# An unused tile of 128 bytes in front of the later working tiles of a two-layer linear-attention and MLP kernel

## The chip, the cores and the metric

The kernel runs on one core of a Trainium2 chip. A core has a matrix engine (TensorE, PE in the profile), three engines for elementwise work (VectorE or DVE, ScalarE or ACT, GpSimd or POOL), and SyncE (SP), which here issues the DMAs. Operands of matmuls lie in SBUF, a memory of 128 partitions in which a tile has one start address for all partitions; results go to PSUM banks. The metric is the time of one execution in microseconds on the device. A matmul reads two operands: the stationary one, which a weight load (PEld in the profile) puts into the array, and the moving one, which streams past it.

## The reference

The input x has 2048 rows of D = 448. Two kinds of block alternate, twice:

```python
def _A_ref(x, wqkv, wo):          # 16 heads of 28
    q, k, v = ...                 # from x @ wqkv
    phi = lambda t: jnp.where(t > 0, t + 1, jnp.exp(t)) + 1e-6
    pq, pk = phi(q), phi(k)
    kv = einsum("bhsd,bhse->bhde", pk, v)
    z = einsum("bhsd->bhd", pk)
    o = einsum("bhqd,bhde->bhqe", pq, kv) / (einsum("bhqd,bhd->bhq", pq, z) + 1e-6)
    return o @ wo
def _B_ref(x, w1, b1, w2, b2):    # F = 1792
    return gelu(x @ w1 + b1) @ w2 + b2

x = x + _A_ref(layernorm(x), wqkv, wo)
x = x + _B_ref(layernorm(x), w1, b1, w2, b2)
# and both once more, with the same weights
```

## The kernel before, in words

All data is float32. A product of two float32 matrices is computed as three one-pass products of type float32r: each operand is split into a high part (a cast, on ACT) and a low part (the rest, on DVE or POOL), and high x high, high x low and low x high are summed in PSUM. The last chunk of 64 columns puts high and low parts into the two halves of 128 rows and needs two products instead of three. A few small products (the sums over rows, the combination of kv with the weights, and the transposes) are plain float32.

Each of the two layers has three stages. The first phase goes over 16 tiles of 128 rows: layernorm, transposition, split into XH and XL, then the products psk (k, function `proj`, L306 to L311), psq (q, same lines) and G (L481 to L485), which accumulates the normalized x against phi(k). The transition forms M from G, wv and wo (kvp, L641; mp, L651), and the first block's attention output and layernorms (o_mm, L732 to L734, whose moving operands are Mh and Ml). The MLP stage goes over four blocks of 512 rows; each has 14 steps. A step computes hp (`mlp1`, L801 to L805: 11 matmuls, stationary w1h, w1l or w1x, moving XH or XL, 512 columns that lie as four runs of 128), gelu, a split into gh and gl, and then y for the step before (`mlp2`, L819 to L821: 12 matmuls, stationary gh or gl, moving w2h or w2l, 448 columns). Between them stand the attention outputs of the next block (op, `oc_mm`, L743 to L747: stationary qh or ql, moving the pieces of M, which live in tiles of the q weights). The order on every engine is written out by hand (ORDER, STEPS, LAUNCH, PLAN) and nothing reorders it.

Tiles come from pools. A pool places its tags in SBUF one behind the other, in the order in which a tag is first asked for; each tag has a fixed number of buffers, and a buffer's size is rounded up to 32 bytes. The pool `consts` comes first, then `wts` with w1h, w1l, w1x, w2h and w2l, then `work`: nine x tiles (tag H) of 1,792 bytes per partition, five tiles of 4,096 bytes (tag S), then the statistics of the layernorm (bst, bmv, bve, brs, three buffers each of at most 24 bytes of content), two tails of 512 bytes, and then all others: the pieces of the k and q weights (tags W0 to W6 and V0 to V6, used later for pq, pz and M), XH and XL (8,192 bytes, two of each), and A, B, E, F, e and xn of 2,048 bytes, from which the split operands xnh, xnl, qh, ql, gh, gl, kh and kl are taken. The last ones are the small denominators dn and rd.

In the built program w1h, w1l, w1x, w2h and w2l start 64 bytes past a multiple of 256, as do the x tiles and the S tiles; rows inside the weights are multiples of 256 bytes apart, so every slice that a product takes keeps that offset. The statistics end at 143,040, which is 192 past a multiple of 256. The tails and everything behind them up to dn have sizes that are multiples of 256 and so start at 192 too.

The program's first calls are these; the tags bst to brs are first asked for in `ln_stats` under `stage_a`, and the tag of the tails in `stage_n`:

```python
    stage_a(0, 0)
    bn = ln_bn(xt[0, 1])
    stage_n(0, 0)
```

Of the kernel before, what the change touches and what calls it, by code (L numbers as in the profile page):

```python
# [9 lines left out]
F32 = mybir.dt.float32  # L10
# [12 lines left out]
def linear_attn_mlp_kernel(  # L23
# [28 lines left out]
    work = ctx.enter_context(tc.tile_pool(name="work", bufs=2))  # L52
# [138 lines left out]
    def ln_bn(xs):  # L191
        st = work.tile([128, 6], F32, name="bst", tag="bst", bufs=3)
        dve.bn_stats(st, xs)
        return st

    def ln_stats(xs, st=None):
        st = ln_bn(xs) if st is None else st
        mv = work.tile([128, 2], F32, name="bmv", tag="bmv", bufs=3)
        dve.bn_aggr(mv, st)
        ve = work.tile([128, 1], F32, name="bve", tag="bve", bufs=3)  # L200
        dve.tensor_scalar(ve, mv[:, 1:2], 1e-5, None, op0=OP.add)  # L201
        rs = work.tile([128, 1], F32, name="brs", tag="brs", bufs=3)
        pool.tensor_tensor(rs, ve, mhalf, op=OP.pow)  # L203
        return xs, mv, rs
# [172 lines left out]
    def stage_a(l, t):  # L377
        sts[l, t] = ln_stats(xt.pop((l, t)))

    def stage_n(l, t):  # L380

        xs, mv, rs = sts.pop((l, t))
        dve.tensor_scalar(xs, xs, mv[:, 0:1], rs, op0=OP.subtract, op1=OP.mult)
        xns[l, t] = xs
        if t < TURNED[l]:
            d = tails[l, t] = work.tile([128, 128], F32, name="tail", tag="tail", bufs=2)
            act.copy(d.rearrange("p (u n) -> p u n", u=2), xs[:, None, TL:].to_broadcast([128, 2, 64]))
# [521 lines left out]


    stage_a(0, 0)
    bn = ln_bn(xt[0, 1])
    stage_n(0, 0)
    split_hi("k", 0, st_k)
# [4 lines left out]
    for l in range(LAYERS):  # L919
# [27 lines left out]
        for tok in ORDER.split():  # L947
            name, j = tok.rstrip("0123456789"), int("0" + tok.lstrip("abcdefghijklmnopqrstuvwxyzQTG"))
# [69 lines left out]
```

## Time and profile before

| | |
|---|---|
| median of 3 runs | 885.9 us (885.64 to 886.61) |
| the profiled execution | 884.81 us |
| its span, first to last instruction | 883.1 us |
| granted clock of TensorE | 1.000 |
| TensorE busy, matmuls | 877.8 us, 4182 records |
| of these y (L819 to L821) | 1344 |
| hp (L801 to L805) | 1232 |
| psk, psq, G | 352 each |
| op (L743 to L747) | 264 |
| VectorE, ScalarE, GpSimd busy | 489.9, 343.5, 220.8 us |

A row of a group gives an engine's instructions of one line of the code. Ends of matmuls are modelled in the profile, and matmuls overlap, so the distance from one start to the next (called pitch below) says what a matmul costs while TensorE is never idle; starts are in the view in order of time. In tile names buffer numbers are left out: y<-w2h,gh is a matmul into y from w2h (moving) and gh (stationary).

### The profile page before, as it was taken

How to read it: one execution, taken by the hardware profiler on the slowest of the kernel's cores; microseconds unless marked ns; L12 is line 12 of the kernel's file. 1: busy time of each engine (PE TensorE's matmuls, PEld its weight loads, DVE VectorE, ACT ScalarE, POOL GpSimd, SP SyncE). 2: the span in 40 equal slices, each digit the busy share in tenths (PEclk: the TensorE clock that was granted, in tenths of full speed). 3: DMA queues.
4: the chain of work that ended last, by engine and by line, in shares of the span. 5: the costliest groups of instructions: out<-in, count | busy, mean ns of one | idle time of the engine just before them, and what ended most of it. 6: DMA issues, size and time to landing. Idle time of an engine off the chain costs nothing.

```text
span 883.1 us, 11676 instructions
## 1 busy us (share of the span) xinstructions
PE 877.8 (99%) x4182; PEld 773.0 (88%) x4182; DVE 489.9 (55%) x953; ACT 343.5 (39%) x603; POOL 220.8 (25%) x250
## 2 busy tenths in 40 slices
PE   9999999999999999999999999999999999999998
PEld 8999888888888888888899998988888888888887
DVE  6878585658455443226477876864664373433112
ACT  5676635334323322333356565332232233233221
POOL 5566532335013102012222344210320140130000
PEclk9999999999999999999999999999999999999999
DMA  5475637633313402051146543352332423111001
GB/s 157 135 231 165 199 88 211 180 99 118 131 59 104 154 0 96 1 178 48 48 133 192 164 127 105 113 171 79 116 106 84 136 72 108 49 48 42 1 1 42
DMA packets 63482, 94.76 MB, mean 107 GB/s; under 512 B 8896, under 2 KB 58560, under 8 KB 63424
## 3 DMA queue, kind: packets, MB, share of 16 engines
q1 hardware_dynamic: 63424, 94.01, 34.0%
q8 instruction: 33, 0.54, 0.3%
q14 instruction: 25, 0.20, 0.1%
HBM read 56.17 MB, written 34.60 MB: 103 GB/s over the span
## 4 chain that ended last, share of the span: by engine, by line
PE 96%; DMA 1%; DVE 1%; ACT 1%; issue 0%; SPq 0%; POOL 0%; DVEq 0%; ACTq 0%; POOLq 0%
PE y L820 10%; PE y L821 10%; PE y L819 10%; PE hp L801 9%; PE hp L803 9%; PE hp L802 9%; PE hp L805 3%; PE hp L804 3%; PE psq L308 2%; PE psq L307 2%; PE psq L306 2%; PE psk L307 2%; PE G L482 2%; PE G L483 2%; PE psk L308 2%; PE G L481 2%
## 5 line engine op out<-in xcount | busy, mean ns | idle before, releaser
L811 DVE TENSOR_TENSOR gl<-g,gh 128x512 fp32r<-128x512 f32 x112 | 83.1, 742 | 306.3 <-ACT gh L810 306.3
L807 ACT ACTIVATE g<-hp,b1s 128x512 f32<-128x512 f32 x112 | 77.2, 689 | 412.5 <-PE hp L805 409.2
L820 PE MATMUL y<-w2l,gh 128*128 128x448 f32 x448 | 164.6, 367 | 0.0
L821 PE MATMUL y<-w2h,gl 128*128 128x448 f32 x448 | 164.0, 366 | 0.0
L819 PE MATMUL y<-w2h,gh 128*128 128x448 f32 x448 | 162.9, 364 | 0.0
L801 PE MATMUL hp<-XH,w1h 128*128 128x512 f32 x336 | 132.8, 395 | 0.0
L803 PE MATMUL hp<-XL,w1h 128*128 128x512 f32 x336 | 132.4, 394 | 0.0
L802 PE MATMUL hp<-XH,w1l 128*128 128x512 f32 x336 | 132.1, 393 | 0.0
L203 POOL TENSOR_TENSOR brs<-bve,mhalf 128x1 f32<-128x1 f32 x64 | 39.5, 617 | 286.5 <-DVE bve L201 283.4
L820 PEld LDWEIGHTS y<-w2l,gh 128*128 128x128 f32 x448 | 84.1, 188 | 10.1
L819 PEld LDWEIGHTS y<-w2h,gh 128*128 128x128 f32 x448 | 84.1, 188 | 9.8
L821 PEld LDWEIGHTS y<-w2h,gl 128*128 128x128 f32 x448 | 84.2, 188 | 6.1
L803 PEld LDWEIGHTS hp<-XL,w1h 128*128 128x128 f32 x336 | 63.1, 188 | 15.1 <-issue 0.5
L802 PEld LDWEIGHTS hp<-XH,w1l 128*128 128x128 f32 x336 | 63.6, 189 | 11.7
L801 PEld LDWEIGHTS hp<-XH,w1h 128*128 128x128 f32 x336 | 63.0, 188 | 11.8
L810 ACT CAST gh<-g 128x512 fp32r<-128x512 f32 x112 | 69.6, 622 | 3.6
L694 POOL TENSOR_TENSOR pz<-pq,zb 128x448 f32<-128x448 f32 x32 | 36.8, 1154 | 87.2 <-DVE dn L700 76.1
L416 POOL TENSOR_TENSOR xnl<-x,xnh 128x384 fp32r<-128x384 f32 x32 | 35.1, 1095 | 71.7 <-ACT xnh L415 39.6
L296 DVE TENSOR_TENSOR XL<-sp,XH 128x512 fp32r<-128x512 f32 x50 | 44.4, 894 | 4.2 <-ACT XH L295 4.2
L805 PE MATMUL hp<-XL,w1x 128*128 128x512 f32 x112 | 44.4, 397 | 0.0
L804 PE MATMUL hp<-XH,w1x 128*128 128x512 f32 x112 | 44.0, 393 | 0.0
L763 POOL TENSOR_TENSOR x<-x,b2b 128x448 f32<-128x448 f32 x32 | 42.0, 1332 | 0.0
(146 smaller groups left out, 1565.0 us busy)
## 6 DMA issues: line engine op xcount, KB each, us to landing
x<-in_A_x_dram SPq DMA_DIRECT2D x32, 224.0 KB, 3.8
pq_d<-eq SPq DMA_DIRECT2D x32, 224.0 KB, 2.9
pq<-pq_d SPq DMA_DIRECT2D x32, 224.0 KB, 3.2
sq_m<-sq SPq DMA_DIRECT2D x14, 512.0 KB, 2.8
sp<-sq_m SPq DMA_DIRECT2D x56, 128.0 KB, 3.0
x<-x_d SPq DMA_DIRECT2D x32, 224.0 KB, 3.4
sq_a<-sq SPq DMA_DIRECT2D x12, 512.0 KB, 2.9
sp<-sq_a SPq DMA_DIRECT2D x48, 128.0 KB, 3.1
```

Of the source, the lines that this page charges most:

```text
L296: eng.tensor_tensor(lo.rearrange("p (c i n) -> p c i n", c=4, n=32), x, f(h), op=OP.subtract)
L801: pe.matmul(o, w1h[:, c, s], x.moving(x.hi, c), start=(c == 0), stop=False)
L802: pe.matmul(o, w1l[:, c, s], x.moving(x.hi, c), start=False, stop=False)
L803: pe.matmul(o, w1h[:, c, s], x.moving(x.lo, c), start=False, stop=False)
L804: pe.matmul(o, w1x[:, s], x.moving(x.hi, 3), start=False, stop=False)
L805: pe.matmul(o, w1x[:, s], x.moving(x.lo, 3), start=False, stop=True)
L807: act.activation(g, hp, AF.Gelu_apprx_tanh, bias=b1s[:, i:i + 1])
L810: act.copy(gh, g)
L811: dve.tensor_sub(gl, g, f(gh))
L819: pe.matmul(acc[j], gh[:, s], w2h[:, i], start=first, stop=False)
L820: pe.matmul(acc[j], gh[:, s], w2l[:, i], start=False, stop=False)
L821: pe.matmul(acc[j], gl[:, s], w2h[:, i], start=False, stop=last)
```

## The change

One line is added behind the first call of `stage_a`. It takes a tile of 32 float32 numbers per partition, 128 bytes, under a tag of its own, and nothing reads or writes it:

```diff
     stage_a(0, 0)
+    work.tile([128, 32], F32, name="space", tag="space", bufs=1)
     bn = ln_bn(xt[0, 1])
     stage_n(0, 0)
     split_hi("k", 0, st_k)
```

In the built program the tile stands between the statistics and the tails, and all that follows starts 128 bytes later: the tails at 143,168, which is 64 past a multiple of 256, and so on. The instructions of every engine, their order and their semaphores are the same as before.

## The prediction

> **What bounds the kernel now.** I read the page's head first, then the chain, then the groups by tile, then the order of time.
>
> ```profile
> span 883.1 us, 11676 instructions
> PE 877.8 (99%) x4182; PEld 773.0 (88%) x4182; DVE 489.9 (55%) x953; ACT 343.5 (39%) x603; POOL 220.8 (25%) x250
> PEclk9999999999999999999999999999999999999999
> ...
> PE 96%; DMA 1%; DVE 1%; ACT 1%; issue 0%; SPq 0%; POOL 0%; DVEq 0%; ACTq 0%; POOLq 0%
> ```
>
> TensorE is busy for 877.8 of 883.1 us at the full granted clock, and 96% of the chain that ended last is its matmuls. So only two things can move the end: the distance from one matmul's start to the next (the pitch, below), or a new wait. Waits of TensorE hardly exist: its view of waits lists 1.1 us for the first warm-up and 0.2 us in one G. The next views are the groups by tile: shortest/median/longest duration in ns, then first and last start.
>
> ```profile
> L819 PE MATMUL y<-w2h,gh x448: 358/364/373, 144.3 to 878.5; 128*128 128x448 f32 x150
> L820 PE MATMUL y<-w2l,gh x448: 358/367/373, 144.5 to 878.7; 128*128 128x448 f32 x150
> L821 PE MATMUL y<-w2h,gl x448: 358/368/373, 144.7 to 878.9; 128*128 128x448 f32 x150
> ```
> ```profile
> L743 PE MATMUL op<-wq,qh x72: 365/369/369, 169.3 to 768.2; 128*128 128x448 f32 x72
> L744 PE MATMUL op<-wq,qh x72: 362/365/366, 169.5 to 768.4; 128*128 128x448 f32 x72
> L745 PE MATMUL op<-wq,ql x72: 362/365/369, 169.7 to 768.6; 128*128 128x448 f32 x72
> ...
> L746 PE MATMUL op<-wq,qh x24: 365/365/365, 171.1 to 768.8; 128*128 128x448 f32 x24
> L747 PE MATMUL op<-wq,ql x24: 365/365/365, 171.3 to 769.0; 128*128 128x448 f32 x24
> ```
> ```profile
> L801 PE MATMUL hp<-XH,w1h x336: 390/392/404, 139.1 to 873.0; 128*128 128x512 f32 x168
> L804 PE MATMUL hp<-XH,w1x x112: 392/392/398, 141.3 to 873.8; 128*128 128x512 f32 x112
> ```
>
> These rows are a comparison that the kernel already contains. The op products run between the y products, in the same stage, with the same shape and the same neighbours on the other engines; but both operands of op (wq streamed; qh or ql loaded as weights) start 192 bytes past a multiple of 256, while y streams w2 from 64 past one and loads gh or gl from 192. The op durations lie in 362 to 369 ns, those of y in 358 to 373: twice as wide, and somewhat longer in the middle. The addresses of the operands do show in TensorE's time, by a little.
>
> Durations are modelled; pitches are not. In order of time (start, duration in us):
>
> ```profile
> 301.38 0.39 PE L803 MATMUL hp<-XL,w1h 128*128 128x512 f32 x1
> 301.61 0.39 PE L804 MATMUL hp<-XH,w1x 128*128 128x512 f32 x1
> 301.84 0.40 PE L805 MATMUL hp<-XL,w1x 128*128 128x512 f32 x1
> 302.08 0.36 PE L819 MATMUL y<-w2h,gh 128*128 128x448 f32 x1
> 302.28 0.36 PE L820 MATMUL y<-w2l,gh 128*128 128x448 f32 x1
> 302.48 0.37 PE L821 MATMUL y<-w2h,gl 128*128 128x448 f32 x1
> 302.69 0.36 PE L819 MATMUL y<-w2h,gh 128*128 128x448 f32 x1
> ```
>
> Starts are 0.20 to 0.24 us apart. Differencing the starts of the whole trace, in ns: y 203.8 (1,343 pitches); op with both operands at 192, 203.25 (264); the k, q and G products of the first phase, also 192 and 192, 203.1 without the pitches over 233, which are waits; hp 232.1 (1,232). The group means say the same: y 365.7 (the mean of 364, 367 and 366), op 365.5, hp 394.2, each its pitch plus 162.
>
> **The change, part by part.** The tile is never written or read, so no instruction, transfer or wait is added, and every engine and queue keeps its order. What moves is addresses. Before the new tile lie the twelve statistics buffers, 32 bytes apart, ending at 192 past a multiple of 256; every later tile up to the last four denominators' (dn, rd) is a multiple of 256 long. The 128 bytes take all of these from 192 to 64: tails, W and V pieces, XH, XL, A, B, E, F, e, xn. w1, w2, the x tiles and the S tiles stay at 64.
>
> So products fall in three classes: mixed 64/192 that become equal (y 1,344, hp 1,232, and 80 of the o products of block 0, whose Mh and part of Ml sit in S tiles), and equal 192/192 that become equal 64/64 (1,336: k, q, G, op and 16 of the o products).
>
> 1. y and the 80 o products: 203.8 to the 203.25 of op, 0.55 ns x 1,424 = 0.8 us gained. All of it is on the path, since TensorE does nothing else.
>
> 2. hp has no row with equal operands, so it is bounded. For what 64 more columns cost I take the two fp32 products: mp, 448 wide, has a pitch of 375.5 ns and kvp, 112 wide, 98.4, so 0.825 ns a column; a y column costs 203.8/448 = 0.455, little over half, so I take half of 0.825, 0.412, or 26.4 ns for 64 columns. If hp with equal operands is op plus that, its pitch is 203.25 + 26.4 = 229.65, and 2.45 ns x 1,232 = 3.0 us is gained. If instead the pitch grows in proportion to the width, 203.25 x 512/448 = 232.3, hp already runs as an equal product would and nothing is gained. Between: op's 0.55 ns, the only price of the offset seen on anything, gives 0.7 us. What is then left above y plus 26.4 (232.1 - 230.2 = 1.9 ns) is due to the offset or to hp's stream in four runs of 128; I give half of it to each, 0.95 ns x 1,232 = 1.2 us. I take 1.9 us, ends 0 and 3.0.
>
> 3. The 1,336 equal products: 192/192 to 64/64. Nearest row: the first-phase ones agree within 0.5 ns whether their operands lie at 192 or at 448 past a multiple of 512. I take nothing; ends are 0.55 ns either way, 0.7 us gained or lost.
>
> 4. The fp32 transposes: the four slices of tq start at 192, 128, 64 and 0 and pitch 108 to 113 ns in any of them. Nothing.
>
> 5. Copies, splits and sums on DVE, ACT and POOL, and the DMAs into W and V: cover is TensorE's own work. One step of the MLP lasts 11 x 232.1 + 12 x 203.8 = 5.0 us against 0.69 + 0.62 + 0.74 = 2.05 us of gelu, copy and split. If that cover were gone it would show as the waits of TensorE above, which hold 1.3 us. Only up to 13 us and where the phases change (around 94, 104 and 537 us) TensorE waits, some 4 us in pitches over 233 together. Loads of tiles at 64 and of tiles at 192 both occur now (x 3.4 us, pq 3.2 us to landing). A tenth of the 4 us either way bounds it; I take nothing.
>
> Sum: -0.8 - 1.9 = -2.7 us. The profiled execution took 884.8 us, its span of 883.1 and 1.7 around it; the change makes it 882.1 with a span of 880.4. It was 1.1 below the median of 885.9 (its runs lie from 885.6 to 886.6), so against that median I say 883.2.
>
> The rows show the neighbour in address mattering by 0.55 ns. [...]
>
> **The rivals.**
>
> A. Nothing measurable. The offset is worth only the 0.8 us of step 1, or op's 203.25 owes something else (its weights change every three products, its stream never repeats a tile at once). For it: the proportional reading of step 2, and 0.55 ns on 203 is small. Against: the doubled spread of y. Time 885.9 - 0.8 + 0.7 to 885.9 - 0.8, say 885.3.
>
> B. Slower: hp's long slot multiplies. Its longest durations, 404 ns against a median of 392, are no scatter. An hp product sums over four chunks of the width of x; the first matmul of the third chunk (L801, c=2) pitches 240.1 in the mean, those of the first two chunks 229.0; so at some distances between stream and weights one matmul in eleven pays 11 ns. With another distance all three chunks may hit it: 2 x 11 x 112 = 2.5 us lost. With step 1's gain of 0.8 that is 887.6. It decides from one added long slot in each step on, 1.2 us, which already eats step 1. Against: equal operands are calmer where they can be seen.
>
> C. More: the long slot goes as well and 64/64 is better than 192/192 too (step 3's end): 885.9 - 0.8 - 3.0 - 0.7 = 881.4. No row has 64/64 products.
>
> D. The change does not do what it says, the tile landing elsewhere or being dropped: addresses as built exclude it, so it gets nothing.
>
> **How the numbers follow.** 0.2%, 1.8 us, is about what a measurement of this kernel can tell from no change. Forecast, hp gaining between 1.0 and 3.0 us: 0.45, 882.1 to 884.1. A: 0.33, all within 0.2%. B: 0.15, half of it over 887.7 or near it, half inside 0.2%. C: 0.07. Faster by over 0.2% is then the forecast, C, less a part that scatters over the edge: 0.49. Slower: half of B and a rest for absolute offsets that I don't see, 0.12. Same: 0.39. The range leaves a tenth out at each end: below, most of C, with 0.3 us for the runs' scatter, 881.5; above, the worse part of B, 887.4. The forecast's own range is 881.8 to 884.4.
>
> **What would show it.** Right: the y rows narrow to about 362 to 369 and their mean falls from 365.7 to 365.2; hp's mean falls from 394.2 to about 392.7, its 404s disappear; op, psk, psq and G stay at 365; no wait of TensorE grows; counts are equal. A is right if y and hp keep their means within 0.3 ns. B is right if L801 gets longer in more chunks. The forecast is wrong above all if hp's excess belongs to its four separate runs of columns and not to its addresses, or if the class 64/64 behaves unlike 192/192.

## The result and the profile after

The changed kernel took 878.7 us (median of six runs; 877.8 to 880.6) against 885.4 us before (now six runs, too; the 885.9 above was the median of three): a ratio of 0.993, 95% interval 0.9915 to 0.9945. That is faster, and by two and a half times what was forecast (6.7 us against 2.7), outside the range. The profiled execution took 877.8 us, its span 876.1.

The head of the page and TensorE's waits after:

```profile
span 876.1 us, 11676 instructions
PE 870.8 (99%) x4182; PEld 771.5 (88%) x4182; DVE 489.0 (56%) x953; ACT 343.3 (39%) x603; POOL 220.8 (25%) x250
```
```profile
PE warm L157 <- DVE ones L152: 1.1, 1, 1.1
PE tp L246 <- DVE x L383: 0.3, 1, 0.3
```

Counts are the same, TensorE still fills the span, and its waits come to 1.4 us against 1.3. Its busy time fell by 7.0 us, as the span did. The groups by tile after (shortest/median/longest duration in ns):

```profile
L819 PE MATMUL y<-w2h,gh x448: 362/365/369, 143.5 to 871.5; 128*128 128x448 f32 x150
L820 PE MATMUL y<-w2l,gh x448: 362/365/369, 143.7 to 871.7; 128*128 128x448 f32 x150
L821 PE MATMUL y<-w2h,gl x448: 362/365/369, 143.9 to 871.9; 128*128 128x448 f32 x150
```
```profile
L801 PE MATMUL hp<-XH,w1h x336: 387/389/396, 138.3 to 866.1; 128*128 128x512 f32 x168
L804 PE MATMUL hp<-XH,w1x x112: 389/389/389, 140.5 to 866.8; 128*128 128x512 f32 x112
```

y narrowed from 358 to 373 down to the 362 to 369 that op had before. hp lost its long slots of 404, and its median fell from 392 to 389; L804 has one duration only. In order of time, a step of hp after:

```profile
302.16 0.39 PE L801 MATMUL hp<-XH,w1h 128*128 128x512 f32 x1
302.39 0.40 PE L802 MATMUL hp<-XH,w1l 128*128 128x512 f32 x1
302.62 0.39 PE L803 MATMUL hp<-XL,w1h 128*128 128x512 f32 x1
302.85 0.39 PE L801 MATMUL hp<-XH,w1h 128*128 128x512 f32 x1
303.08 0.39 PE L802 MATMUL hp<-XH,w1l 128*128 128x512 f32 x1
303.31 0.39 PE L803 MATMUL hp<-XL,w1h 128*128 128x512 f32 x1
303.53 0.39 PE L801 MATMUL hp<-XH,w1h 128*128 128x512 f32 x1
303.76 0.39 PE L802 MATMUL hp<-XH,w1l 128*128 128x512 f32 x1
```

Two decimals hide the pattern; the mean distances of starts over all 112 steps show it. The three matmuls of the first chunk are 231.0, 233.2 and 230.1 ns apart, the next two 228.1 and 227.9, and the last six settle at 226.4 to 227.0. Before, the step never settled: 228.8 to 233.1 all along, and 240.1 at the first matmul of the third chunk.

Pitches (distance of starts, in ns, means over the whole trace; single pitches over 250 at 448 columns and over 260 at 512, some 30 that stand at waits, behind float32 products or at the start of a phase, left out):

| products | before | after |
|---|---|---|
| hp, 1,232 | 232.0 | 228.2 |
| y, 1,344 | 203.8 | 202.7 |
| op, 264 | 203.25 | 202.3 |
| psk, psq, G | 203.0, 203.6, 202.8 | 203.0, 203.7, 203.1 |

With those put back, hp's pitches sum to 286.0 us before and 281.5 after, those of all 448-wide float32r products to 565.4 and 563.6. That is 4.5 + 1.8 = 6.3 us. The other 0.7 of the 7.0 lies ahead of the first product of k, which started at 6.8 us instead of 7.4, and is no part of the change: the first hp, at 139.1 us before and 138.3 after, started at 138.3 too with w1 and w2 moved alone (below), which gained nothing, and at 139.2 with everything moved, which gained as much as the change.

### The profile page after: what moved, and what is told of

Read it like the earlier page. It is cut to its first block, busy times and chain, and to the rows that moved or that the text cites. A ratio compares the mean times of both kernels' runs of the same rounds, so it can differ in the third digit from the quotient of the medians.

```text
span 876.1 us, 11676 instructions
## 1 busy us (share of the span) xinstructions
PE 870.8 (99%) x4182; PEld 771.5 (88%) x4182; DVE 489.0 (56%) x953; ACT 343.3 (39%) x603; POOL 220.8 (25%) x250
## 4 chain that ended last, share of the span: by engine, by line
PE 98%; DVE 0%; DMA 0%; POOL 0%; ACT 0%; issue 0%; DVEq 0%
PE y L821 10%; PE y L819 10%; PE y L820 10%; PE hp L802 9%; PE hp L803 9%; PE hp L801 9%; PE hp L805 3%; PE hp L804 3%; PE psk L307 2%; PE G L482 2%; PE psq L306 2%; PE psq L307 2%; PE psq L308 2%; PE G L481 2%; PE G L483 2%; PE psk L308 2%
## 5 line engine op out<-in xcount | busy, mean ns | idle before, releaser
L804 PE MATMUL hp<-XH,w1x 128*128 128x512 f32 x112 | 43.6, 389 | 0.0
L193 DVE BATCH_NORM_STATS2 bst<-x 128x6 f32<-128x448 f32 x64 | 39.9, 624 | 4.8 <-DMA x<-in_A_x_dram 3.7
```

The lines of the kernel that those rows point to most:

```text
L804: pe.matmul(o, w1x[:, s], x.moving(x.hi, 3), start=False, stop=False)
```

## Experiments

"Difference" below is the start of the moving operand less the start of the stationary one, modulo 256 bytes. hp had 128 before (192 and 64), and y had 128 too (64 and 192); the change makes both 0.

### Is it the place modulo 256? Other lengths of the tile

```diff
-    work.tile([128, 32], F32, name="space", ...)
+    work.tile([128, 64], F32, name="space", ...)     # 256 bytes; 96: 384; 16: 64; 48: 192
```

256 bytes:

> The tile has 256 bytes instead of 128: everything behind it moves, but keeps its place modulo 256. Theory 1 (what counts is the difference of the starts of the moving and the stationary operand modulo 256): as before the change, ratio 1.000 (885.4 us), y durations 358 to 373 ns, mean 365.7, hp mean 394.2. Theory 2 (the place as such matters: a period longer than 256, or a distance between tiles): a ratio below 0.996 or above 1.004. Theory 3 (any tile between the statistics and the rest separates them and that is what helps): 0.993.

384 bytes:

> 384 bytes: the same place modulo 256 as with the change, another modulo 512. Theory 1: as with the change, ratio 0.993 (878.7 us), y mean 365.3, hp 390.6. Theory 2: anything else; with a period of 512 bytes not 0.993.

64 bytes:

> 64 bytes: the later tiles start at multiples of 256, 64 below the offset of w1, w2. Theory 1 in its strict form (only equal offsets help): ratio 1.000 or above, hp mean 394 or more. Theory 1 by distance (half the distance, half the loss): about 0.9965 (882 us), hp mean near 392.4. Products with both operands among the later tiles (op, psk, psq, G) stay at 365 to 366 by either.

192 bytes:

> 192 bytes: the later tiles start 64 above the offset of w1, w2. Strict form: ratio 1.000 or above, hp mean 394 or more. By distance: about 0.9965, and equal to the tile of 64 bytes. If the sign of the difference matters (stationary ahead of or behind the moving operand) this and the tile of 64 bytes differ by more than 0.002.

| tile | difference hp, y | ratio to before (95%) | hp | y | psk, G |
|---|---|---|---|---|---|
| 256 | 128, 128 | 1.0002 (0.9993 to 1.0012) | 232.0 | 203.8 | 204.0, 203.7 |
| 384 | 0, 0 | 0.9921 (0.9906 to 0.9935) | 228.15 | 202.8 | 202.9, 203.1 |
| 64 | 192, 64 | 0.9997 (0.9988 to 1.0007) | 233.2 | 201.2 | 205.0, 204.6 |
| 192 | 64, 192 | 0.9988 (0.9979 to 0.9997) | 230.6 | 202.4 | 206.1, 205.8 |

A tile of 256 bytes left hp, y and the total as they were, and one of 384 did what 128 does: 256 bytes more moved hp and y by no more than 0.1 ns, and separating the tiles is not the cause. But the last two rows don't follow theory 1 in either form. y was faster with the difference 64 (201.2) than with 0 (202.7), so equal was not best for it. The sign mattered, too: hp has 233.2 and 230.6, y 201.2 and 202.4 with the same two differences the other way round. The two totals hide this; they differ by 0.0009, less than the 0.002 that was to tell. And psk and G, whose two operands stay equal, got 2 to 3 ns slower, and 1 ns slower even with 256 bytes, where no tile's place modulo 256 has moved. So these two hung on something else as well, which comes up again below.

### Difference or place? w1 and w2 moved, too

```diff
+    wts.tile([128, 32], F32, name="wpad")
     w1h = wts.tile([128, 3, F], F32R, name="w1h")
```

This alone:

> A tile of 128 bytes ahead of w1 instead: w1, w2, x and S at 192, all later tiles at 64. The later tiles have the places of the change, but hp and y stay mixed, the other way round (hp streams from 64 and loads from 192; y streams from 192 and loads from 64). If the difference decides: as before, 885.0 us, ratio 1.000, hp 232, y 203.8. If the place of XH, XL, A and B decides: as with the change, 0.993.

With the tile of the change as well:

> Both tiles: everything at 192, as far behind each other as with the change. If the difference decides: ratio 0.993, hp 228.2, y 202.7. If the place at 64 decides: 1.000. Products at equal offsets were up to 2 ns slower at 0 and 128 than at 64 and 192, so a part may hang on the place modulo 128, which is the same for 64 and 192.

Alone: ratio 0.9999 (0.9989 to 1.0008). With both: 0.9932 (0.9917 to 0.9947). The hp groups of the two:

```profile
L802 PE MATMUL hp<-XH,w1h x336: 390/392/404, 138.3 to 872.3; 128*128 128x512 f32 x168
L805 PE MATMUL hp<-XH,w1x x112: 392/392/398, 140.5 to 873.0; 128*128 128x512 f32 x112
```
```profile
L802 PE MATMUL hp<-XH,w1h x336: 387/389/397, 139.2 to 867.0; 128*128 128x512 f32 x168
L805 PE MATMUL hp<-XH,w1x x112: 389/389/389, 141.4 to 867.7; 128*128 128x512 f32 x112
```

The first (all later tiles at 64, as with the change, but w1 at 192) is the kernel before again, with its 404s; the second, with everything at 192, is the changed kernel. Slot by slot along the step the means agree within 0.2 ns with those of the kernel they resemble. For hp and y the difference counted here and not the place: with 192/64 in place of 64/192 the time was that of before (0.9999), with 192/192 in place of 64/64 that of the change (0.9932 against 0.993).

### One kind of product at a time

```diff
         xn = xns.pop((l, t))
+        if (l, t) == (0, 0):
+            work.tile([128, 32], F32, name="space2", tag="space2", bufs=1)
         h = t512("A", 2, "xnh", F32R)
```

With the tile of the change (hp equal, y mixed):

> The tile of the change, and a second one of 128 bytes ahead of A: XH, XL, W and V at 64 as with the change, A, B, E, F and e back at 192. hp is equal (64/64), y mixed (64/192), op mixed, psk and psq equal, G equal at 192. If the pitch belongs to each product's own two operands: hp 228.2 ns, y 203.8, gain against before 1,232 x 3.8 = 4.7 us, about 880.4, ratio 0.9947. If the neighbours or the place of the whole decide, hp does not get its 228.

Without it (y equal, hp mixed):

> Only the tile of 128 bytes ahead of A: A, B, E, F and e at 64, XH, XL, W and V at 192 as before. y equal (64/64), hp mixed. By own operands: y 202.75 ns, hp 232.0, gain 1,344 x 1.05 = 1.4 us, about 883.7, ratio 0.9984; the gains of this run and of the one with hp alone add up to that of the change (6.1 us of pitches).

Ratios 0.9979 (0.997 to 0.9989) and 1.0034 (1.0021 to 1.0047). Neither expectation held. With hp equal alone hp pitched 229.8, not 228.2: the seventh to tenth matmul of its step are at 226.6 to 226.9, as with the change, but the six ahead of them, behind the mixed y, at 228 to 236. With y equal alone y pitched 204.7, slower than the mixed 203.8, and the first phase rose as well: psk to 206.25, psq to 205.0, G to 205.7, though both operands of psk lie just where they lay before. Its groups there, and those before:

```profile
L306 PE MATMUL psk<-wk,XH x96: 362/368/473, 7.5 to 534.7; 128*128 128x448 f32 x96
L307 PE MATMUL psk<-wk,XH x96: 362/368/475, 7.8 to 534.9; 128*128 128x448 f32 x96
```
```profile
L306 PE MATMUL psk<-wk,XH x96: 362/365/467, 7.4 to 531.8; 128*128 128x448 f32 x96
L307 PE MATMUL psk<-wk,XH x96: 358/365/473, 7.8 to 532.0; 128*128 128x448 f32 x96
```

So a product's own two addresses did not fix its pitch (psk: 203.0 before, 206.25 here); what ran around it had a say.

### w1l alone moved away

```diff
+    wts.tile([128, 32], F32, name="lpad0")
     w1l = wts.tile([128, 3, F], F32R, name="w1l")
+    wts.tile([128, 32], F32, name="lpad1")
     w1x = wts.tile([128, F], F32R, name="w1x")
...
+    work.tile([128, 32], F32, name="space", tag="space", bufs=1)
```

> The changed kernel with w1l alone moved to 192 (128 bytes ahead of it and 128 behind). In hp, L801 streams XH while the w1l for L802 is being loaded; L802 has the w1l as its own weights and streams XH while the w1h for L803 is loaded. If a stream collides with the load that runs under it, L801 gets longer (from 227 ns in the steady chunks to 229 or more) and L802 does not. If a product's own pair decides, L802 gets longer and L801 does not. If both or all three change, the pattern of the whole step decides. y stays at 202.7. Whole: 0.994 to 0.996.

Ratio 0.9958 (0.9943 to 0.9973). In the second and third chunk the product ahead of w1l went from 228.1 and 226.8 to 231.7 and 232.1, the one with w1l from 227.9 and 227.0 to 233.4 and 233.8, the third from 226.5 and 226.4 to 227.6 and 227.7; the fourth chunk, where w1l has no part, stayed at 226.6 and 226.7. The product ahead of w1l, under which w1l is loaded (in the profile after the load starts 2 to 4 ns behind that product's start and takes 188 ns), paid 4 to 5 ns and the one that uses it 6 to 7, and the loop was back within 1.3 ns right behind them. (In the first chunk, which had not settled, the one with w1l fell from 233.2 to 231.8.) By the expectation this is the third case, the pattern of the whole step; which of the two reads, stream or load, is held up is not told by it.

### Do the four runs of hp's stream cost anything?

```diff
-            return x.rearrange("p (t c n) -> p t c n", t=4, c=4)[:, :, c]
+            return x.rearrange("p (c t n) -> p c t n", t=4, c=4)[:, c]
```

On the kernel before:

> The kernel before, with hp streaming one run of 512 columns of XH or XL in place of four runs of 128 (it takes 512 neighbouring columns, which are other elements, so what hp computes is changed; the sizes, the counts and the offset 192 stay). If half of hp's excess belongs to the four runs, as the prediction took it, hp falls from 232.0 to about 231 ns. If it is all the offset, hp stays at 232.0. If it is all the runs, about 230.

On the changed kernel:

> The same edit (hp computes with other elements of XH and XL) on the changed kernel, offset 64. If the runs cost something with equal offsets too, hp falls from 228.2 below 227.5; if they cost nothing, it stays at 228.2, of which the first chunk holds 231 and the rest 227.

In one execution of each, hp pitched 232.0 and 228.2, as without the edit. The four runs cost nothing that shows; what hp lost with the change was the offset's.

### Series of equal products, without neighbours

```diff
+    def series(n, cols, k, at, width=128):
+        o = bank("m", 2, "sr")
+        for i in range(n):
+            pe.matmul(o[:width, :cols], st4[:, at + k * 8:at + k * 8 + width], mv4[:, at:at + cols],
+                      start=True, stop=True)
```

> The changed kernel with 41 series of 40 one-pass products added behind its last product, into a PSUM bank that nothing reads: stream from w2h, weights from w1h shifted by 0 to 7 steps of 32 bytes, 448 and 512 columns; three series with both operands moved together by 64, 128 and 192; and series with loads of 64 and of 32 columns in place of 128. Theory of the load under the stream: the pitch depends on the difference in steps, is the same for equal operands wherever they lie, and the dependence gets weaker or goes with loads of 64 and 32 columns. Theory of the product's own start (stream and weights, without the load): the same dependence with the narrower loads. If the entry decides (two pitches for one difference), the series with difference 0 that follow different series differ: 202.7 or 206.7.

(There were 39 series, not 41.) Behind the kernel's last work no other engine is busy and the DMAs are still, so what these series show is TensorE's alone:

```profile
core 0: us, PE busy (x) PEld busy (x) DVE busy (x) ACT busy (x) POOL busy (x), PEclk, DMA share, GB/s
900.00:1100.00 200.00, 200.00 (x920) 172.42 (x919) 0.00 (x0) 0.00 (x0) 0.00 (x0) 1.00 0.00 1
```

Mean pitch in ns of each series of 40, without its first four; st4 is w1h and mv4 w2h:

| difference | 0 | 32 | 64 | 96 | 128 | 160 | 192 | 224 |
|---|---|---|---|---|---|---|---|---|
| 448 columns | 202.7 | 206.7 | 200.1 | 205.3 | 204.0 | 200.0 | 202.1 to 202.3 | 204.4 |
| 512 columns | 226.7 to 227.4 | 233.3 | 228.9 to 229.0 | 233.4 | 232.4 | 234.3 | 233.4 | 233.4 |

Both operands moved on together by 64, 128 and 192 gave 202.7 each at 448 columns: place alone made no difference there. Second series of most of these differences, in the next experiment, agree within 0.3 ns. The kernel's pitches are in this table: y and hp with 128 (203.8 and 232.0), y and hp with 0 (202.7 and 227 once settled), y with 64 (200.1, below). The groups of three of these series, 448 columns at the differences 0, 128 and 64, show the rows of y in their three forms:

```profile
L998 PE MATMUL sr<-w2h,w1h x34: 362/365/369, 873.2 to 879.9; 128*128 128x448 f32 x34
```
```profile
L998 PE MATMUL sr<-w2h,w1h x33: 358/367/373, 881.3 to 887.8; 128*128 128x448 f32 x33
```
```profile
L998 PE MATMUL sr<-w2h,w1h x34: 360/362/363, 913.7 to 920.3; 128*128 128x448 f32 x34
```

In the table the dependence is not smooth and is another one for each of the two widths; inside a series the pitches repeat: 199, 207, 202, 203, 202 over and over with difference 0, steady 200 with 160, steady 206.7 with 32. Loads of 64 and 32 columns in place of 128, with a load time of 134 and 108 ns in place of 188, gave 202.3 and 202.1 at difference 0, 202.6 and 202.3 at 128, 201.6 and 206.7 at 64, 203.4 and 206.7 at 192. The four differences lie within 3.9 ns of each other with 128 columns, 1.8 with 64 and 4.6 with 32: the shorter loads changed the pattern, and did not make it fade. The theory that the time of the load under the stream is what costs is not borne out; the product's own start alone does not fit either, since the width of the load changed the pattern.

### One loop, two steady states

```diff
+    for k in range(8):
+        series(21, 512, k)
+        series(40, 448, 0)
+        series(20, 512, k)
+        series(40, 448, 0)
```

(and likewise behind 448-wide series and transposes)

> The changed kernel with series behind its last product, into a bank that nothing reads: 40 equal products of 448 columns (difference 0), each time entered from another series: from 448 columns at the differences 32, 224, 160 and 96, from 20 or 21 products of 512 columns at all eight differences, and from one to three transposes. If a loop of equal products has two steady states, some of these series stay at 206.7 for all their 40 products and the others at 202.7. If it has one, all are at 202.7 after a few products, and the 205 to 207 of the first phase in the other kernels comes from something outside TensorE's two operands.

The same 40 products of difference 0 settled on 202.7 or on 206.7 and stayed there. Behind 448 columns at difference 32 it was 206.7; behind 224, 160 and 96, 202.7. Behind 512 columns: 206.7 after 192 and after 96 with either count; after 160 with 21 products ahead but not with 20; after 128 with 20 but not with 21; never after 0, 224, 64 and 32. Behind one to three transposes it was 202.7. Two of these series, behind 21 and behind 20 products at 160:

```profile
L998 PE MATMUL sr<-w2h,w1h x34: 363/368/368, 1004.2 to 1011.0; 128*128 128x448 f32 x34
```
```profile
L998 PE MATMUL sr<-w2h,w1h x34: 362/365/369, 1017.3 to 1024.0; 128*128 128x448 f32 x34
```

368 is the median that psk had in the run with y alone. So these equal products had two pitches, 202.7 and 206.7, and what ran just before them decided. The kernels show the same. In the run with y alone, behind a mixed hp, the group of y at 145.0 us pitches 203, 207, 203, 202, 203, 199 and so on, and the next one, at 150.0 us, 207, 206, 207, 207, 206, 207 to its end; without their first two pitches, 51 of 110 groups are above 206 in the mean and the rest at about 203, so 204.7 is a mixture. In the changed kernel, where hp has the difference 0, none of the 110 is above 203.3. The first phase is such a mixture as well: of 31 unbroken groups of psk, 2 are above 206 before the change and 2 after it, 9 with the tile of 256 bytes, 17 with 64, 26 with 192 and 29 with y alone.

What holds the first phase at the longer pitch in some kernels was asked with V6, the one mixed operand there in the run with y alone, put back to 192:

```diff
+        if (name, c) == ("q", 3):
+            work.tile([128, 32], F32, name="space3", tag="space3", bufs=1)
         hi = piece(name, c if c < 3 else 6)
...
+        if (l, t) == (0, 0):
+            work.tile([128, 32], F32, name="space4", tag="space4", bufs=1)
         kh = t512("E", 2, "kh", F32R)[:, :D]
```

> The run with y alone, with V6 put back to 192 by 128 bytes ahead of it and 128 behind it: the last chunk of q, the only mixed product of the first phase there, becomes equal. If one mixed product in a group holds the others at 207: psk and psq fall from 206.3 and 205.2 to 203, G from 205.7 to 203. If they stay at 205 to 207, the mixed product was not it, and the passage between products at 64 and products at 192 remains.

psk 206.2, psq 205.4, G 205.5 in one execution: V6 was not it. y pitched 203.4 there against 204.7, with 20 groups above 206 against 51, though hp and y lie as in the run with y alone. Which entry leads to which pitch in the kernel stays open.

### Versions by the table

A and B at 0, so that y and G get the difference 64, and hp keeps 0:

```diff
+    work.tile([128, 32], F32, name="space", ...)     # ahead of the tails
+    work.tile([128, 48], F32, name="space2", ...)    # ahead of A
+    work.tile([128, 16], F32, name="space3", ...)    # ahead of V6
```

> The tile of the change, 192 bytes ahead of A and 64 ahead of V6: hp, psk, psq and op equal at 64 as with the change; A and B at 0, so that y streams from 64 and loads from 0, and G streams kh from 64 and loads xnh from 0. In the run with the tile of 64 bytes y had this difference and pitched 201.2. If what counts is the difference modulo 256 and best for y is 64 and not 0: y 201.2, G near 201, 1,344 x 1.6 + 360 x 1.9 = 2.8 us below the changed kernel, about 875.5, ratio 0.989. If hp needs the step's other products to be equal too, hp rises above 228.2 and the ratio is 0.993 or worse.

873.7 us, ratio 0.9874 (0.9857 to 0.989): y 200.1, G 200.3, and hp went down too, from 228.2 to 227.1, since behind these y its first chunk is hardly slower than the rest (228.8, 227.0 and 228.0 against 226.7). Its y rows:

```profile
L823 PE MATMUL y<-w2h,gh x448: 362/363/363, 144.8 to 867.3; 128*128 128x448 f32 x150
L824 PE MATMUL y<-w2l,gh x448: 360/360/363, 145.0 to 867.5; 128*128 128x448 f32 x150
```

Then V0 to V5 at 128 (64 bytes ahead of V0, 128 ahead of A, 64 ahead of V6), and last the same 64 bytes moved up ahead of W1:

> The version with A and B at 0 (873.7 us), with V0 to V5 at 128 in addition: psq streams from 128 and loads from 64, op of the later blocks streams from 128 and loads from 64, so both get the difference 64 that made y 200.1 and G 200.3. By that rule psq and op fall from 203.4 and 202.2 to about 200.5: (288 + 216) x 2.5 = 1.3 us, ratio 0.986. If the difference 64 owes its 200 ns to the loop of y and G alone, 0.9874 or worse.

> The version with A and B at 0 and V0 to V5 at 128, its 64 bytes moved up ahead of W1, so that W1, W2, W4, W5 and W6 are at 128 too: 8 of the 11 psk products get the difference 64. By the table psk falls from 204 to about 201.5, 352 x 2.6 = 0.9 us, time about 872.0, ratio 0.985. If the step between the two kinds inside a psk group costs as much as it gains, 0.986 as without it.

872.9 us, 0.9859 (0.9842 to 0.9875), with psq 200.6 and op 200.9 where they have 64; and 871.0 us, 0.9838 (0.9822 to 0.9855), with psk 200.5 where it has 64. The intervals of the first two of these three versions overlap, so their order rests on the pitches. The last is the fastest version of the study: 14 us below the kernel before and some 8 below the changed one, with the same instructions in the same order.

## Why the prediction was wrong

The direction and the mechanism were right: only addresses move, TensorE's pitch is the path, y narrows to 362 to 369, hp loses its 404s, no wait grows to speak of. The sizes were not. That equal offsets are calmer held for 0 against 128 at both widths (202.7 against 204.0 ns, 226.7 to 227.4 against 232.4), but as a rule it was luck: at 448 columns the differences 64 and 160 beat 0 (200.1 and 200.0).

Step 1 (y and the o products, 0.55 ns each): mis-sized. y gained 1.05 ns, 1.4 us; the o products of block 0 gained nothing (203.9 before, 204.3 after). The op row was no clean sample of equal products. It stood between mixed hp and mixed y, and with the same equal offsets it fell itself from 203.25 to 202.3 once its neighbours were equal; the series puts equal products at 202.7.

Step 2 (hp, 1.9 us with ends 0 and 3.0) is the step that failed: 3.8 ns and 4.6 us, above its upper end. Three things in it were off. The floor of 229.65 was built on op's 203.25, 0.6 too high. The 26.4 ns for 64 columns came from fp32 products; the series has 226.7 less 202.7, so 24.0. These two together put the settled pitch of an equal hp at 226.7, and with a slower first chunk 228.2 in the mean. And half of the 1.9 ns that was left over went to the four runs of 128; the runs cost nothing that shows (232.0 and 228.2 with one run as with four). The bound took for the price without the offset's cost one that had some of that cost in it.

Step 3 (1,336 products that stay equal, nothing): held for k, q and G, 202.8 to 203.7 before and after, but not for the reason given; op, which it counts in, fell by 0.9 ns, 0.2 us. Agreement at 192 and 448 modulo 512 said nothing on other entries; in four of the experiments equal products of the first phase ran at 204.5 to 206.3.

Steps 4 and 5 (transposes and the other engines, nothing): held. Waits of TensorE went from 1.3 to 1.4 us.

Rival A, nothing measurable, was wrong: y fell by 1.05 ns and hp by 3.8, and the series have 200.0 to 206.7 ns at 448 columns and 226.7 to 234.3 at 512 by the difference alone. Whether it is the load's reading that meets the stream, no run here shows. Rival B, the long slot multiplying, was wrong for this change: the slot went. Rival C had the long slot going and 64/64 better than 192/192. Its time of 881.4 was still too high, and its second half is refuted: all at 192 was as fast as all at 64 (0.9932 against 0.993). Rival D was rightly excluded: the addresses as built have hp and y at the difference 0.

The chances said faster at 0.49; the range ended at 881.5, 2.8 us above the result. Of these, 1.6 are what step 2's end lacked, 0.6 what step 1 lacked, and 0.5 is no part of the change: the median before came out that much lower with six runs than with three.

## What to carry to other kernels

Where TensorE is never idle, look at the spread of the durations in a group, not only at its mean: 358 to 373 beside 362 to 369 for the same shape was the sign, and the place of a tile modulo 256 bytes was worth 0.7%, a chosen place 1.6%. A row that is to serve as the price without a cost must come from a loop that is free of that cost in its neighbours too (op, equal all along, fell from 203.25 to 202.3 with its neighbours); where none exists, a short series of the product by itself, behind the kernel's end, gives it in one run (here 202.7 and 226.7). Equal offsets were no rule here: the table by difference and width has 200.1 at 64 against 202.7 at 0, y and G at 64 took the time to 0.9874, from 0.993 with the change, and an aligned part beside an unaligned one lost (y alone: 1.0034).

## What the runs showed that was not expected

The pitch of a float32r product hung here on the difference of its operands' starts, in steps as small as 32 bytes and not smoothly: at 448 columns 200.1 at 64 stands beside 206.7 at 32. 256 bytes more changed nothing that shows (hp 232.0 and y 203.8 with the tile of 256 bytes, as before). The best difference was another at each of the two widths (64 or 160 at 448 columns, 200.1 and 200.0; 0 at 512, 226.7 to 227.4). And one and the same loop had two steady states, 202.7 and 206.7 ns, chosen in two cases by a single product more or less ahead of it (20 or 21 of 512 columns at 160 and at 128). Why is not settled: the experiments separate place from difference and exclude the four runs (232.0 and 228.2 without them, too), and with nothing else running the series (0.00 us busy on DVE, ACT and POOL) leave no other engine as the cause, but neither the length of the load nor its neighbour told what happens inside TensorE or its memory.
